# Two batches' scan blocks per burst of small products, from the fifth block on

## The chip, the cores and the metric

One core of one Trainium2 chip. The metric is the device time of one execution in microseconds (us), as the median over the executions of a kernel. The profile is of one execution; its span is some 2 us shorter than the device time. A program on one core has no second die to compare with. Of six timed executions of a kernel here often one is 2 to 4 us longer than the rest, for some kernels with a mean granted TensorE clock of 0.995 to 0.996 in place of 1.0; medians are little touched by them. One run in all was far slower: of the seven executions of the kernel before that were timed with probe, moved and late, one took 443.3 us at a mean clock of 0.852; it is marked slow and left out of the ratios. In the lines shown, PE is TensorE's passes, PEld its weight loads, DVE VectorE, ACT ScalarE, POOL GpSimd, SP SyncE.

## The reference, cut to what matters

A chunked scan (Mamba-2 style) over 4 batches, 8 heads, 768 tokens, head width 32 and state width 16, followed by a feed-forward layer with an ELU between its two large products. All fp32.

```python
for c in range(nc):                      # chunks of 32 in the reference, 64 in the kernel
    cum = np.cumsum(la, axis=-1)
    L = np.exp(cum[:, :, :, None] - cum[:, :, None, :]) * causal
    M = np.einsum('bhin,bhjn->bhij', Cc, Bc) * L             # "scores", weighed
    y_intra = np.einsum('bhij,bhjd->bhid', M, xc)            # "inside"
    y_inter = np.einsum('bhin,bhnd->bhid', Cc, state) * np.exp(cum)[..., None]   # "across"
    state = decay_full * state + np.sum(Bx, axis=2)          # "sums", "states"
# then, on x of 3072 tokens by 256:
h = x @ w_in                                                 # 256 -> 2048, called l1 below
g = np.where(h > 0, h, np.exp(np.minimum(h, 0)) - 1)         # elu
out = g @ w_out                                              # 2048 -> 256, called l2 below
```

## The kernel before: the parts that the change and the argument touch

The 3072 tokens are 12 blocks of 256. The large products (l1 and l2) of one block are interleaved with the small products of the scan of a later block. A group of l1 or of l2 is eight large passes. Each block has bursts of small products: scores (16 products of 32 rows by 64 columns of the array), sums (12 or 16, on 64 by 32), across (12 or 16, on 32 by 64) and inside (32, on 64 by 32). An fp32 product shows in the trace as two weight loads and two passes, so 16 products are "x32". A turn transposes B and C of a block by four more passes, and a bank here is the buffer that one of TensorE's output tiles takes; a large group waits where another engine has yet to read it (0.40 us for VectorE at 51.59 us in the changed kernel).

```python
def scores(n):
    gs = [psum([P, 2, 2, Q], "ps_g") for _ in range(4)]
    for u in range(2):
        for v in range(2):
            for q in range(4):
                rows, toks = slice(32 * q, 32 * q + 32), slice(Q * v, Q * v + Q)
                nc.tensor.matmul(out=gs[q][toks, u], lhsT=s["bt"][rows, u, toks],
                                 rhs=s["ctm"][rows, u, :, toks], ...)
# ... cut: sums, states, across, inside are built alike, one block at a time
def meet(n):
    across(n)
    inside(n)
    if n + 1 < NP:
        sums(n + 1)
        states(n + 1)
# ... cut
for n in range(2, NP):
    for i in range(8):
        l2(n - 2, i)
        l1(n, i)
        while lag:
            elu()
        # ... cut: loads, decays, turns of block n + 2, block 3's special case
        if i == 6 and n + 1 < NP:
            meet(n + 1)
        if i == 7 and n + 2 < NP:
            scores(n + 2)
            for q in range(4):
                weigh(n + 2, q)
```

## Time and profile before

| | before |
|---|---|
| device time, median | 390.22 us (3 runs, 390.02 to 393.0) |
| profiled span | 388.0 us |
| large passes of TensorE | 1536, 215.8 ns each: 331.5 us |
| first to last large pass | 370.9 us, so 39.6 us go to everything else in between |

The prediction below shows the lines on TensorE. What the other engines do in time is in the busy tenths of the 40 slices (9 is 90% or more of a slice of 9.7 us):

```profile
DVE  4877867943323232323123233223232321221000
ACT  3969879662653563563554464455366234334000
```

The reader is to see that VectorE (DVE) is 60% to over 90% busy only in slices 2 to 8 (some 10 to 78 us), where it also converts the weights; this is where a change of its load can reach TensorE. Behind that it is some 20 to 40% busy.

The blocks of 256 instructions that the prediction and the runs speak of: on the page 28 packets of 16 KB went over the instruction queue, and the trace records 7193 instructions of TensorE, 257 to a packet. In the changed kernel the last three of its 28 packets start behind 6553, 6809 and 7065 recorded instructions, so 256 apart. A packet takes 0.88 to 1.45 us, 1.01 in the median.

A way of reading that carries this whole document: the large passes are the same in every version, so I add up, pass by pass, how much longer than 215.8 ns it took from each large pass to the next. Everything that a burst, a wait or a stop costs is in that sum, called **lost time** below. A burst's cost is the gap that it leaves plus 0.104 us, by which the second large pass behind any burst comes late.

### The profile page before, as it was taken

What the parts mean: (1) busy time and instruction counts of PE and PEld (TensorE: products, weight loads), DVE (VectorE), ACT (ScalarE), POOL (GpSimd) and SP (SyncE); (2) the same over time, 40 slices, a digit from 0 to 9 for tenths busy, and PEclk for the clock granted to TensorE, in tenths of its full rate; (3) what the DMA queues carried; (4) which work ended last, traced back from release to release, by engine and by line L of the source; (5) the groups of instructions that cost most, each with busy time, mean ns of one, the idle gap of its engine ahead of it and who ended that gap; (6) DMA issues with size and microseconds to landing.
All of it is one profiled execution on the core that took longest, in us unless ns stands there. A gap on an engine that the chain in (4) does not pass through costs nothing.

```text
span 388.0 us, 8744 instructions
## 1 busy us (share of the span) xinstructions
PE 381.7 (98%) x3546; PEld 323.8 (83%) x3546; DVE 136.8 (35%) x280; ACT 200.1 (52%) x480; POOL 73.0 (19%) x133
## 2 busy tenths in 40 slices
PE   8999999999999999999999999999999999999996
PEld 4678788888888888888888888888888888888885
DVE  4877867943323232323123233223232321221000
ACT  3969879662653563563554464455366234334000
POOL 6525426540120120011021012012012000000000
DMA  8979966016007007006105303402500000000000
GB/s 165 225 165 256 280 157 119 7 37 113 4 12 133 7 3 137 14 2 123 28 0 88 65 0 53 101 0 45 95 2 29 2 0 11 20 2 27 0 29 27
DMA packets 86921, 25.02 MB, mean 64 GB/s; under 512 B 77184, under 2 KB 81504, under 8 KB 86880
## 3 DMA queue, kind: packets, MB, share of 16 engines
q1 hardware_dynamic: 84704, 24.26, 29.7%
q8 instruction: 28, 0.46, 0.5%
q10 hardware_dynamic: 2176, 0.20, 0.4%
q14 instruction: 13, 0.11, 0.1%
HBM read 21.10 MB, written 3.34 MB: 63 GB/s over the span
## 4 chain that ended last, share of the span: by engine, by line
PE 83%; ACT 5%; DMA 3%; SPq 3%; DVE 3%; issue 1%; POOL 0%; DVEq 0%; ACTq 0%; POOLq 0%
PE ps_o L552 38%; PE ps_h L525 36%; PE ps_o L567 4%; PE ps_y L497 2%; ACT L L393 2%; SPq L107 2%; PE ps_g L412 1%; DMA w<-in_moe_w_in_dram 1%; PE ps_y L482 1%; DMA xr<-in_x_dram 1%; ACT e L537 1%; DMA flat<-F 1%; PE ps_st L438 1%; ACT mag L152 1%; SPq L115 1%
## 5 line engine op out<-in xcount | busy, mean ns | idle before, releaser
L525 PE MATMUL ps_h<-yT,w_in 128*128 128x256 f32 x768 | 181.3, 380 | 1.1 <-DVE g L539 0.5
L552 PE MATMUL ps_o<-w_out,g 128*128 128x256 f32 x704 | 167.3, 382 | 0.1
L525 PEld LDWEIGHTS ps_h<-yT,w_in 128*128 128x128 f32 x768 | 145.5, 190 | 22.0 <-ACT yT L508 0.9
L552 PEld LDWEIGHTS ps_o<-w_out,g 128*128 128x128 f32 x704 | 131.7, 190 | 19.5 <-issue 1.4
L539 DVE SCALAR_TENSOR_TENSOR g<-e,ps_h 128x512 f32<-128x512 f32 x96 | 65.9, 687 | 209.7 <-ACT e L538 209.6
L537 ACT ACTIVATE e<-ps_h 128x512 f32<-128x512 f32 x96 | 57.1, 595 | 137.2 <-PE ps_h L525 137.0
L538 ACT ACTIVATE e<-e 128x512 f32<-128x512 f32 x96 | 60.5, 630 | 3.0
L398 POOL TENSOR_SCALAR_AFFINE_SELECT L<-L 64x512 f32<-64x512 f32 x40 | 26.6, 665 | 132.4 <-ACT L L393 131.2
L393 ACT ACTIVATE L<-L,ncum 128x64 f32<-128x64 f32 x160 | 41.9, 334 | 0.0
L508 ACT COPY yT<-ps_y 64x128 f32<-64x128 f32 (+1 forms) x70 | 17.9, 260 | 6.7 <-PE ps_y L497 5.7
L459 POOL TENSOR_TENSOR Sx<-S_new,hmask 128x64 f32<-128x64 f32 x44 | 13.3, 304 | 20.8 <-DVE S_new L454 14.1
L421 DVE TENSOR_TENSOR M<-ps_g,L 128x256 f32<-128x256 f32 x48 | 17.1, 416 | 0.1
L558 ACT COPY ob<-ps_o 128x512 f32<-128x512 f32 x11 | 6.4, 585 | 18.4 <-PE ps_o L552 18.4
L321 POOL TENSOR_TENSOR sc<-bc,eb 128x256 f32<-128x256 f32 x12 | 7.8, 656 | 38.9 <-DMA bc<-in_B_dram 37.2
L567 PE MATMUL ps_o<-w_out,g 128*128 128x256 f32 x64 | 14.0, 379 | 0.0
L567 PEld LDWEIGHTS ps_o<-w_out,g 128*128 128x128 f32 x64 | 12.2, 190 | 1.6
L194 POOL TENSOR_TENSOR w_out<-mag,w_out 128x512 uint32<-128x512 uint32 x8 | 10.2, 1274 | 16.5 <-DVE mag L184 16.5
L194 POOL TENSOR_TENSOR w_in<-mag,w_in 128x512 uint32<-128x512 uint32 x8 | 10.2, 1277 | 15.2 <-DVE mag L184 15.2
L184 DVE SCALAR_TENSOR_TENSOR mag<-mag,sgn 128x512 uint32<-128x512 uint32 x16 | 12.3, 772 | 0.5
L454 DVE SCALAR_TENSOR_TENSOR S_new<-S_new,ec,ps_st 128x64 f32<-128x64 f32 x40 | 11.2, 279 | 2.5
L152 ACT ACTIVATE mag<-w 128x512 f32<-128x512 f32 x16 | 10.7, 671 | 1.5 <-DMA w<-in_moe_w_in_dram 1.3
L497 PE MATMUL ps_y<-M,xr 64*32 64x64 f32 x768 | 10.6, 225 | 0.0
(67 smaller groups left out, 137.5 us busy)
## 6 DMA issues: line engine op xcount, KB each, us to landing
L<-flat SPq DMA_DIRECT2D x20, 256.0 KB, 4.5
w<-in_moe_w_in_dram SPq DMA_DIRECT2D x8, 512.0 KB, 5.0
w<-in_moe_w_out_dram SPq DMA_DIRECT2D x8, 512.0 KB, 6.4
xr<-in_x_dram SPq DMA_DIRECT2D x24, 128.0 KB, 4.4
out_dram<-ob SPq DMA_DIRECT2D x11, 256.0 KB, 2.2
bc<-in_B_dram SPq DMA_DIRECT2D x24, 64.0 KB, 3.2
bc<-in_C_dram SPq DMA_DIRECT2D x22, 64.0 KB, 3.4
ec<-flat_exp SPq DMA_DIRECT2D x64, 16.0 KB, 1.8
```

The source lines that it names most:

```text
L194: nc.gpsimd.tensor_tensor(out=w, in0=w_mag[i][:, :, cols], in1=w, op=ALU.add)
L393: nc.scalar.activation(L[:, h, u], L[:, h, u], ACT.Exp, bias=ncum[:, u, row:row + 1])
L398: nc.gpsimd.affine_select(out=part, in_=part, pattern=[[0, 4], [0, 2], [1, Q]], compare_op=ALU.is_ge, fill=0.0, base=0, channel_multiplier=-1)
L421: nc.vector.tensor_tensor(out=M, in0=s["g"][q], in1=s["L"][:, 2 * q:2 * q + 2].rearrange("p k u i -> p u k i"), op=ALU.mult)
L497: nc.tensor.matmul(out=s["y"][t][v][col:col + D, u], lhsT=s["x"][toks, u, D * h:D * (h + 1)], rhs=s["M"][h // 2][toks, u, h % 2], start=Fa ...
L508: nc.scalar.copy(out=yT[n][at:at + count, t, :, Q * v:Q * v + Q], in_=s["y"][t][v][src:src + count])
L525: nc.tensor.matmul(out=ps[:, j], lhsT=w_in[:, k, m * P:(m + 1) * P], rhs=yT[n][:, k].rearrange("p u i -> p (u i)"), start=(k == 0), stop=( ...
L537: nc.scalar.activation(e, ps, ACT.Relu, scale=-1.0)
L538: nc.scalar.activation(e, e, ACT.Exp, scale=-1.0)
L539: nc.vector.scalar_tensor_tensor(out=g_of[n][:, 2 * i:2 * i + 2], in0=e, scalar=1.0, in1=ps, op0=ALU.subtract, op1=ALU.max)
L552: nc.tensor.matmul(out=o_of[n][:, ts], lhsT=g_of[n][:, m, ts * P:(ts + 1) * P], rhs=w_out[:, m], start=(m == 0 and ts == 0), stop=(m == MC ...
L567: nc.tensor.matmul(out=ps, lhsT=g_of[n][:, m, ts * P:(ts + 1) * P], rhs=w_out[:, m], start=(m == 0), stop=(m == MC - 1))
```

## The change

Its intent: fewer edges. A burst of small products costs TensorE time at its two ends (0.33 us in the kernel before) and at each change of tile shape inside it (0.14 to 0.19 us); blocks 4 to 11 are taken as four pairs of two batches at the same position, with one burst for scores and sums of both and one for across and inside of both. The places of the second burst are set by hand in a table ("placed by the count of TensorE's instructions"). The diff, cut to its core:

```diff
+    def place(n):
+        return 2 * (n // (2 * NG)) + n % 2, n // 2 % NG      # two batches side by side
-    def scores(n):
+    def scores(*ns):
-        s["g"] = gs = [psum([P, 2, 2, Q], "ps_g") for _ in range(4)]
+        gs = [psum([P, len(ns), 2, 2, Q], "ps_g") for _ in range(4)]
+        for at, n in enumerate(ns):
     # ... cut: the same for sums, across, inside
-    def meet(n): ...
-            first_exp(3)                       # block 3's exponent as a product
+            spread_exp(3)                      # ... by DMA (issued earlier, s == 8)
+    ends = {(3, 14): 4, (5, 10): 6, (7, 13): 8, (9, 9): 10}
+    def end_of_two(n, step):
+        m = ends.get((n, step))
+        if m:
+            inside(across(m, m + 1), m, m + 1)
     # ... cut: order of loads and turns
+            if 4 <= m < NP and n % 2 == 1:
+                if i == 2:
+                    scores(m, m + 1)
+                    sums(m, m + 1)
+                    for q in range(4):
+                        weigh(m, q)
+                        weigh(m + 1, q)
+                    states(m)
+                    states(m + 1)
+            end_of_two(n, 2 * i + 1)
```

By the new numbering block 1 is the first block of the second batch (before, the second block of the first), and block 2 has four chunks to sum where it had three.

More of the change, by code (lines that the diff above doesn't have):

```diff
@@ L70 @@
     const = ctx.enter_context(tc.tile_pool(name="const", bufs=1))
-    raw = ctx.enter_context(tc.tile_pool(name="raw", bufs=4))
+    raw = ctx.enter_context(tc.tile_pool(name="raw", bufs=3))
     att = ctx.enter_context(tc.tile_pool(name="att", bufs=2))
@@ L95 @@
     st = {}
+    def place(n):
+        return 2 * (n // (2 * NG)) + n % 2, n // 2 % NG
     def rows_of(n):
-        b, g = divmod(n, NG)
+        b, g = place(n)
         return slice(BH * g + NH * b, BH * g + NH * (b + 1))
     def load_bc(n, c_queue=nc.sync):
-        b, g = divmod(n, NG)
+        b, g = place(n)
         st.setdefault(n, {})["bc"] = raw.tile([P, 2, 2, NH, N], F32, tag="bc", name="bc")
@@ L110, in load_x @@
     def load_x(n):
-        b, g = divmod(n, NG)
-        st[n]["x"] = raw.tile([P, 2, NH * D], F32, tag="xr", name="xr")
+        b, g = place(n)
+        st[n]["x"] = raw.tile([P, 2, NH * D], F32, tag="xr", name="xr", bufs=4)
         for u in range(2):
@@ L150, in w_abs @@
     def w_abs(i):
-        w_mag[i] = conv.tile([P, 2, CW], U32, tag="mag", name="mag", bufs=3)
+        w_mag[i] = conv.tile([P, 2, CW], U32, tag="mag", name="mag")
         nc.scalar.activation(w_mag[i].bitcast(F32), w_words(i)[1].bitcast(F32), ACT.Abs)
@@ L198 @@
     w_load(0)
-    idle = const.tile([P, 4, P], BF16, name="idle")
+    idle = att.tile([P, 4, P], BF16, tag="M", name="idle", bufs=8)
     nc.vector.memset(idle, 0.0)
@@ L242 @@
         out=minus, in0=ident, scalar1=-1.0, scalar2=None, op0=ALU.mult)
-    heads = [const.tile([ROWS, NH, N], F32, name=f"heads{n}") for n in range(4)]
-    for n in range(4):
+    heads = [const.tile([ROWS, NH, N], F32, name=f"heads{n}") for n in range(3)]
+    for n in range(3):
         nc.gpsimd.tensor_copy(
@@ L400, in decay @@
                     compare_op=ALU.is_ge, fill=0.0, base=0, channel_multiplier=-1)
-    def scores(n):
-        s = st[n]
-        s["g"] = gs = [psum([P, 2, 2, Q], "ps_g") for _ in range(4)]
-        for u in range(2):
-            for v in range(2):
-                for q in range(4):
-                    rows, toks = slice(32 * q, 32 * q + 32), slice(Q * v, Q * v + Q)
-                    nc.tensor.matmul(
-                        out=gs[q][toks, u], lhsT=s["bt"][rows, u, toks],
-                        rhs=s["ctm"][rows, u, :, toks], start=True, stop=True,
-                        tile_position=(32 * q, Q * v), skip_group_check=True)
-        s["M"] = []
+    def scores(*ns):
+        gs = [psum([P, len(ns), 2, 2, Q], "ps_g") for _ in range(4)]
+        for at, n in enumerate(ns):
+            s = st[n]
+            for u in range(2):
+                for v in range(2):
+                    for q in range(4):
+                        rows, toks = slice(32 * q, 32 * q + 32), slice(Q * v, Q * v + Q)
+                        nc.tensor.matmul(
+                            out=gs[q][toks, at, u], lhsT=s["bt"][rows, u, toks],
+                            rhs=s["ctm"][rows, u, :, toks], start=True, stop=True,
+                            tile_position=(32 * q, Q * v), skip_group_check=True)
+            s["g"], s["M"] = [g[:, at] for g in gs], []
     def weigh(n, q):
@@ L426, in chunks, with sums @@
     def chunks(n):
-        return [(u, v) for u in range(2) for v in range(2) if n % NG < NG - 1 or u + v < 2]
-    def sums(n, pool=p_a, tag="a"):
-        s = st[n]
-        s["st"] = ps = [psum([P, 2, 2 * D], "ps_st"),
-                        pool.tile([P, 2, 2 * D], F32, tag=tag, name="ps_st")]
-        for u, v in chunks(n):
-            toks = slice(Q * v, Q * v + Q)
-            for q in range(4):
-                nc.tensor.matmul(
-                    out=ps[v][32 * q:32 * q + 32, u],
-                    lhsT=s["sc"][toks, u, 2 * q:2 * q + 2].rearrange("p h n -> p (h n)"),
-                    rhs=s["x"][toks, u, 2 * D * q:2 * D * (q + 1)], start=True, stop=True,
-                    tile_position=(Q * v, 32 * q), skip_group_check=True)
+        return [(u, v) for u in range(2) for v in range(2)
+                if place(n)[1] < NG - 1 or u + v < 2]
+    def sums(*ns, pool=p_a, tag="a"):
+        ps = [psum([P, len(ns), 2, 2 * D], "ps_st"),
+              pool.tile([P, len(ns), 2, 2 * D], F32, tag=tag, name="ps_st")]
+        for at, n in enumerate(ns):
+            s = st[n]
+            for u, v in chunks(n):
+                toks = slice(Q * v, Q * v + Q)
+                for q in range(4):
+                    nc.tensor.matmul(
+                        out=ps[v][32 * q:32 * q + 32, at, u],
+                        lhsT=s["sc"][toks, u, 2 * q:2 * q + 2].rearrange("p h n -> p (h n)"),
+                        rhs=s["x"][toks, u, 2 * D * q:2 * D * (q + 1)], start=True, stop=True,
+                        tile_position=(Q * v, 32 * q), skip_group_check=True)
+            s["st"] = [p[:, at] for p in ps]
     def states(n):
-        b, g = divmod(n, NG)
+        b, g = place(n)
         s = st[n]
@@ L456, in states @@
                     in1=add, op0=ALU.mult, op1=ALU.add)
-            Sx = att.tile([P, 2, D], F32, tag="Sx", name="Sx", bufs=8)
+            Sx = att.tile([P, 2, D], F32, tag="Sx", name="Sx", bufs=12)
             nc.gpsimd.tensor_tensor(
@@ L462, in states, with across @@
             at = 2 * u + v + 1
-            starts[n + at // 4, at % 4 // 2, at % 2] = Sx
+            starts[n + at // 4 * 2, at % 4 // 2, at % 2] = Sx
     def shift(n, v):
         return 2 * D * v if n else 0
-    def across(n):
-        s = st[n]
-        s["y"] = y = [[psum([P, 2, Q], "ps_y") for _ in range(2)] for _ in range(2)]
+    def across(*ns):
+        y = [[psum([P, len(ns), 2, Q], "ps_y") for _ in range(2)] for _ in range(2)]
         for u in (1, 0):
-            for v in range(2):
-                Sx = starts.pop((n, u, v), None)
-                if Sx is None:
-                    continue
-                for q in range(4):
-                    rows, col = slice(32 * q, 32 * q + 32), (64 * q + shift(n, v)) % P
-                    nc.tensor.matmul(
-                        out=y[q // 2][v][col:col + 64, u],
-                        lhsT=Sx[rows].rearrange("p k d -> p (k d)"),
-                        rhs=s["cts"][rows, u, Q * v:Q * v + Q], start=(u == 1), stop=False,
-                        tile_position=(32 * q, col), skip_group_check=True)
@@ L488, in inside @@
-    def inside(n, ts=(0, 1)):
-        s = st[n]
-        for t in ts:
-            for u in range(2):
+            for at, n in enumerate(ns):
                 for v in range(2):
-                    toks = slice(Q * v, Q * v + Q)
+                    Sx = starts.pop((n, u, v), None)
+                    if Sx is None:
+                        continue
                     for q in range(4):
-                        h, col = 4 * t + q, (D * q + shift(n, v)) % P
+                        rows, col = slice(32 * q, 32 * q + 32), (64 * q + shift(n, v)) % P
@@ L497, in inside @@
                         nc.tensor.matmul(
-                            out=s["y"][t][v][col:col + D, u],
-                            lhsT=s["x"][toks, u, D * h:D * (h + 1)],
-                            rhs=s["M"][h // 2][toks, u, h % 2], start=False, stop=True,
-                            tile_position=(Q * v, col), skip_group_check=True)
-            if t == 0:
-                yT[n] = ffn.tile([P, KC, 2, P], F32, tag="yT", name="yT")
+                            out=y[q // 2][v][col:col + 64, at, u],
@@ new lines, in across, with inside @@
+                            lhsT=Sx[rows].rearrange("p k d -> p (k d)"),
+                            rhs=st[n]["cts"][rows, u, Q * v:Q * v + Q],
+                            start=(u == 1 and at == 0), stop=False,
+                            tile_position=(32 * q, col), skip_group_check=True)
+        return y
+    def inside(y, *ns):
+        for t in range(2):
+            for at, n in enumerate(ns):
+                s = st[n]
+                for u in range(2):
+                    for v in range(2):
+                        toks = slice(Q * v, Q * v + Q)
+                        for q in range(4):
+                            h, col = 4 * t + q, (D * q + shift(n, v)) % P
+                            nc.tensor.matmul(
+                                out=y[t][v][col:col + D, at, u],
+                                lhsT=s["x"][toks, u, D * h:D * (h + 1)],
+                                rhs=s["M"][h // 2][toks, u, h % 2], start=False, stop=True,
+                                tile_position=(Q * v, col), skip_group_check=True)
+            n = ns[0]
+            if n // 2 not in yT:
+                yT[n // 2] = ffn.tile([P, KC, 2, 2, P], F32, tag="yT", name="yT")
+            out = yT[n // 2][:, t, n % 2:n % 2 + len(ns)]
@@ L508, in inside @@
                     nc.scalar.copy(
-                        out=yT[n][at:at + count, t, :, Q * v:Q * v + Q],
-                        in_=s["y"][t][v][src:src + count])
-        if 1 in ts:
+                        out=out[at:at + count, :, :, Q * v:Q * v + Q],
+                        in_=y[t][v][src:src + count])
+        for n in ns:
             st.pop(n)
@@ L526, in l1 @@
                     out=ps[:, j], lhsT=w_in[:, k, m * P:(m + 1) * P],
-                    rhs=yT[n][:, k].rearrange("p u i -> p (u i)"),
+                    rhs=yT[n // 2][:, k, n % 2].rearrange("p u i -> p (u i)"),
                     start=(k == 0), stop=(k == KC - 1))
@@ L541, in elu, with row_of @@
             op0=ALU.subtract, op1=ALU.max)
+    def row_of(n):
+        b, g = place(n)
+        return b * S + g * BLK
     o_of = {}
@@ L558, in l2 @@
             nc.scalar.copy(out=ob, in_=o_of.pop(n))
+            r0 = row_of(n)
             nc.sync.dma_start(
-                out=out[n * BLK:(n + 1) * BLK, :].rearrange("(t p) e -> p t e", p=P), in_=ob)
+                out=out[r0:r0 + BLK, :].rearrange("(t p) e -> p t e", p=P), in_=ob)
     def l2_last(n):
@@ L571, in l2_last @@
             nc.scalar.copy(out=ob[:, ts], in_=ps)
-            r0 = n * BLK + ts * P
+            r0 = row_of(n) + ts * P
             nc.sync.dma_start(out=out[r0:r0 + P, :], in_=ob[:, ts])
-    def meet(n):
-        across(n)
-        inside(n)
-        if n + 1 < NP:
-            sums(n + 1)
-            states(n + 1)
     def w_take(i, low):
@@ L619 @@
     turn_exp(0)
-    sums(0, p_o, "o")
+    sums(0, pool=p_o, tag="o")
     first_minus(*first)
@@ L634 @@
         weigh(0, q)
-    nc.gpsimd.tensor_copy(F[3 * BH:4 * BH, 0], F[BH:2 * BH, 0])
-    second = (1, 0, 1), (1, 1, 3)
+    second = (1, 0, 0), (1, 1, 3)
     first_low(1, 0)
@@ L641 @@
     w_low(1, nc.scalar)
-    across(0)
-    inside(0)
+    inside(across(0), 0)
     w_sign(1)
@@ L672 @@
     scores(1)
-    sums(1, p_o, "o")
+    sums(1, pool=p_o, tag="o")
     weigh(1, 0)
@@ L681 @@
     w_take(4, nc.vector)
-    across(1)
-    inside(1)
+    inside(across(1), 1)
     ncum = turned(F[0:ROWS, 0], "ncum", -1.0, nc.vector)
@@ L714 @@
             load_x(3)
+            spread_exp(3)
             weigh(2, 2)
             weigh(2, 3)
-            sums(2, p_o, "o")
+            sums(2, pool=p_o, tag="o")
             states(2)
         if s == 10:
-            across(2)
-            inside(2)
+            inside(across(2), 2)
         if len(lag) > 1:
             elu()
-    spread_exp(4)
+    ends = {(3, 14): 4, (5, 10): 6, (7, 13): 8, (9, 9): 10}
[3 more added lines that the diff above has]
+            inside(across(m, m + 1), m, m + 1)
     for n in range(2, NP):
@@ L730 @@
                 w_take(todo, nc.vector)
+            end_of_two(n, 2 * i)
             l1(n, i)
@@ L737 @@
                 elu()
-            if i == 0:
-                if n + 2 < NP:
-                    load_bc(n + 2)
-                    spread_cum(n + 2)
-                    load_x(n + 2)
-                if n + 3 < NP:
-                    spread_exp(n + 3)
             if n == 2:
@@ L757 @@
                         weigh(3, q)
-            if n + 2 < NP:
-                if i == 1:
-                    scaled(n + 2, nc.gpsimd)
-                if i == 3:
-                    turn(n + 2)
-                    turn_exp(n + 2)
-                if 2 <= i < 6:
-                    decay(n + 2, i - 2)
-            if i == 4 and n == 2:
-                sums(3)
-                states(3)
-            if i == 6 and n + 1 < NP:
-                meet(n + 1)
-            if i == 7 and n + 2 < NP:
-                scores(n + 2)
-                for q in range(4):
-                    weigh(n + 2, q)
+                if i == 4:
+                    sums(3)
+                    states(3)
+            if n == 2 and i == 6:
+                inside(across(3), 3)
+            m = n + 2 + n % 2
+            if 4 < m < NP and n % 2 == 1 and i in (4, 5):
+                spread_cum(m + i - 4)
+            m = n + 2 - n % 2
+            if 4 <= m < NP and n % 2 == 0:
+                if i < 2:
+                    if m == 4:
+                        spread_cum(m + i)
+                    load_bc(m + i)
+                    spread_exp(m + i)
+                if i == 2:
+                    load_x(m)
+                    load_x(m + 1)
+                if i >= 2:
+                    decay(m + i // 6, (i - 2) % 4)
+                if i in (5, 7):
+                    turn(m + i // 7)
+                    turn_exp(m + i // 7)
+            if 4 <= m < NP and n % 2 == 1:
+                if i < 2:
+                    decay(m + 1, i + 2)
+                    scaled(m + i, nc.gpsimd)
+                if i == 2:
+                    scores(m, m + 1)
+                    sums(m, m + 1)
+                    for q in range(4):
+                        weigh(m, q)
[3 more added lines that the diff above has]
+            end_of_two(n, 2 * i + 1)
     for i in range(8):
```

## The prediction

> **What bounds the kernel now.** I read the page's engine totals first, then the chain that ended last, then the waits of the two TensorE rows in the steady part (88 to 357 us), then TensorE's timeline there.
>
> ```profile
> PE 381.7 (98%) x3546; PEld 323.8 (83%) x3546; DVE 136.8 (35%) x280; ACT 200.1 (52%) x480; POOL 73.0 (19%) x133
> PE   8999999999999999999999999999999999999996
> ...
> PE 83%; ACT 5%; DMA 3%; SPq 3%; DVE 3%; issue 1%; POOL 0%; DVEq 0%; ACTq 0%; POOLq 0%
> ```
>
> TensorE is busy in every slice and the chain is TensorE for 83%; no other engine is above 52%. A busy TensorE may still wait inside, so the waits of its weight loads between 88 and 357 us:
>
> ```profile
> PEld ps_y L482 <- issue: 2.6, 8, 0.3
> PEld ps_g L412 <- issue: 2.3, 7, 0.3
> PEld ps_o L552 <- issue: 1.2, 7, 0.2
> ```
>
> That is the whole list: nobody waits for another engine, a DMA or a buffer (the matmul row itself lists no wait at all). Each of these stops is at an edge between the large products and the small ones. The timeline of one steady period (start, length, line, shapes, passes):
>
> ```profile
> 128.99 1.89 PE L525 MATMUL ps_h<-yT,w_in 128*128 128x256 f32 x8
> 130.71 0.38 PE L331 MATMUL ps_tb<-ident,bc 128*128 128x128 f32 x2
> 130.93 0.38 PE L331 MATMUL ps_tc<-ident,bc 128*128 128x128 f32 x2
> 131.15 1.89 PE L552 MATMUL ps_o<-w_out,g 128*128 128x256 f32 x8
> 132.88 1.89 PE L525 MATMUL ps_h<-yT,w_in 128*128 128x256 f32 x8
> ...
> 139.79 1.89 PE L525 MATMUL ps_h<-yT,w_in 128*128 128x256 f32 x8
> 141.61 0.49 PE L482 MATMUL ps_y<-cts,Sx 32*64 32x64 f32 x32
> 142.02 0.89 PE L497 MATMUL ps_y<-M,xr 64*32 64x64 f32 x64
> 142.71 0.52 PE L438 MATMUL ps_st<-xr,sc 64*32 64x64 f32 x32
> 143.15 2.00 PE L552 MATMUL ps_o<-w_out,g 128*128 128x256 f32 x8
> 144.99 1.89 PE L525 MATMUL ps_h<-yT,w_in 128*128 128x256 f32 x8
> 146.81 0.69 PE L412 MATMUL ps_g<-ctm,bt 32*64 32x128 f32 x32
> ```
>
> A group of eight large passes takes 1.727 us (131.15 to 132.88), so 215.8 ns a pass. What a burst of small products costs is the distance of the large groups around it less two groups. The meeting (across, inside, sums): 144.99 - 139.79 - 3.454 = 1.75 us. The scores: the next L525 group starts at 149.26, so 149.26 - 144.99 - 3.454 = 0.82 us. The turn: 132.88 - 128.99 - 3.454 = 0.44 us. Two more cases, a meeting without sums and sums alone:
>
> ```profile
> 322.96 1.89 PE L525 MATMUL ps_h<-yT,w_in 128*128 128x256 f32 x8
> 324.78 0.49 PE L482 MATMUL ps_y<-cts,Sx 32*64 32x64 f32 x32
> 325.20 0.89 PE L497 MATMUL ps_y<-M,xr 64*32 64x64 f32 x64
> 326.01 1.99 PE L552 MATMUL ps_o<-w_out,g 128*128 128x256 f32 x8
> 327.84 1.89 PE L525 MATMUL ps_h<-yT,w_in 128*128 128x256 f32 x8
> ...
> ```
>
> Meeting without sums: 327.84 - 322.96 - 3.454 = 1.43 us, so sums behind inside add 0.32. Sums alone (L525 groups at 70.79 and 74.82): 4.03 - 3.454 = 0.58 us. The same 16 products thus cost 0.26 us more when they have edges of their own. The edges, from single starts in the trace: the first small product comes 0.31 us after the last large one instead of 0.216 (0.09 lost); between across and inside, where the tile changes from 32 rows by 64 columns to 64 by 32, the next start waits 0.145 (some 0.14 lost); from inside to sums, same tile, 17 ns; after the last small one the first large pass waits 0.15 (0.20 after scores) and the second comes 0.104 late. So in and out cost about 0.33, a change of tile inside a burst 0.14 to 0.19.
>
> [...] 0.14 us at the change of tile, 17 ns where only the data changes. [...] The page shows an instruction queue with 28 packets and 0.46 MB, 16 KB each, 0.5% of 16 engines' 388 us, so 1.1 us each; no burst of before shows a stall from it. [...]
>
> **The change part by part.** Order of instructions and diff say that the large products (1536 passes, 331.5 us) stay. Blocks 0 to 3 run singly as before. Blocks 4 to 11 become four pairs of two batches at the same position, each with one burst scores+sums and one burst across+inside: two bursts per pair for four.
>
> Before, blocks 4 to 11: eight scores at 0.82 = 6.55; meetings 4 to 11 at 1.66, 1.75, 1.75, 1.66, 1.75, 1.75, 1.66 (sums of three chunks: 0.09 less) and 1.43 = 13.4; block 4's sums behind meeting 3, 0.32. Together 20.25 us.
>
> After, scores+sums of a pair: in 0.09; single scores take 0.42 to the last start, and each further round of eight passes 0.109, four more for the second block: 0.86; change of tile 0.20; sums alone take 0.385 from first start to the next large one, plus 0.32 for the second block, plus 0.10 late second pass. Sum 1.96; pairs 4 and 10 have three chunks, 1.78. Across+inside: 1.43, plus four more rounds of across at 0.058 = 0.23, plus 64 more inside passes at 10.6 ns = 0.68: 2.34. Four pairs: 2*1.96 + 2*1.78 + 4*2.34 = 16.85 us. Gain 3.40 us.
>
> Block 3's exponent comes by DMA, so two passes of L311 go: its turn costs 0.87 (62.62 - 58.29 - 3.454), a turn without them 0.44; gain 0.43. Block 2 sums four chunks instead of three: loss 0.09. Turns, transposes and large products: none. Total 3.74 us, all on the path, as TensorE sets the end.
>
> Beside other work: copies of y double in width but halve in number (six of about 0.36, the mean of a 128x256 copy, for twelve of 0.26): ScalarE is freer. The copy of F (0.48, GpSimd) and one of heads (0.45) go, in the start, where TensorE hardly waits for them (0.3 us in the waits). Fewer buffers (bc 3, mag 2): the sum that frees a mag ends about a step before the second next one wants it (POOL sum at 67.6 to 68.9, ACT abs at 71.2), so no wait.
>
> **The rivals.** (1) VectorE's queue after the pair burst becomes the bound. It does 8 weighings of 0.416 and up to 8 states of 0.279, 5.6 us in a row behind one elu that ends some 2.1 us after the burst's start: 7.7 us. The shortest distance to across is the last pair's: 1.96 + four groups of 1.73 = 8.7 us, and that pair has 6 states (7.1, with the last mask on GpSimd 7.6). Margin about 1 us; the banks for the l1 groups in between come free by 5.5. If it failed, up to 1 us lost, in one pair. (2) Instruction fetch: across+inside of a pair is 96 products, each two loads and two passes, 384 instructions in 2.2 us; a burst of before has at most 256. If a whole block of 256 lies in it (1.6 us at this rate), a fetch that takes 1.1 us after being asked for and issued may come late, by my estimate up to 0.4 us, at most 1.6 over four pairs. Counting after's instructions, the bursts start at 0.83, 0.20, 0.89 and 0.13 of a block (origin unknown): near one phase, so the author has placed them to avoid it, as the title says. I give it 0.15 us. (3) DMA: L, bc, ec of two blocks come together, ec's 8 small ones in 5 to 6 us of SyncE; 16 us for a pair of which the last is wanted 24 us after. DMA is busy for 26% there. Hidden. In the third block of steps (53 to 80 us), where VectorE is 90% busy, a late ec of block 3 could hold VectorE's queue: up to 1 us. (4) The gain could be larger if single bursts pay a ramp that a double one does not: at most some tenths.
>
> **Range and chances.** 390.22 - 3.74 + 0.15 = 386.6 us. If every edge saving is halved and one rival takes 0.5 it is 388.5; if all goes well and the start gains 0.7 it is 385.5. For 2% faster TensorE would have to save 7.8 us; the bursts of blocks 4 to 11 are 20 us in all and their products stay, so 2%. For 2% slower a new wait of 11 us would be needed: 2%.
>
> **What would show it.** Right: eight bursts in the steady part; scores+sums 1.9 to 2.0 (1.8), across+inside 2.3 to 2.4 us by the same subtraction; the "issue" waits of L482's and L412's successors in number halved; turn of block 3 at 0.44; span near 384.3. Wrong: a wait of across for the GpSimd mask or VectorE, gaps inside a burst with no releaser (fetch), a first l1 of a pair waiting for ScalarE's yT, or a start (to 53 us) that moves by more than 0.5 us.

## The result, and the profile after

The changed kernel took 387.91 us in the median of 6 runs (387.49 to 388.39), before 390.35 us (6 runs, 390.02 to 393.0). Ratios are computed from the mean time of one kernel's fast runs over that of the other's fast runs of the same rounds, so they are not quite the ratio of the medians quoted: 0.9926, 95% interval 0.9899 to 0.9953. That is faster by 0.7%, "same" at the mark of 2%, and inside the predicted range, 1.3 us above the predicted time. The profiled span is 385.5 us.

First the page's totals and the chain that ended last:

```profile
PE 378.7 (98%) x3544; PEld 324.1 (84%) x3544; DVE 136.9 (36%) x280; ACT 196.7 (51%) x455; POOL 72.1 (19%) x131
...
PE 88%; ACT 4%; DMA 3%; SPq 3%; issue 1%; DVE 0%; ACTq 0%
```

TensorE was busy for 381.7 us and is for 378.7; it still sets the end. Then the waits of the weight loads between 88 and 357 us (waited for, total, times, longest), which is again the whole list, and the matmul row has none:

```profile
PEld ps_y L490 <- issue: 1.3, 4, 0.3
PEld ps_g L417 <- issue: 1.3, 4, 0.3
PEld ps_st L445 <- POOL sc L325: 0.7, 4, 0.2
```

At the way into a burst there are eight stops in place of 15. The third line names GpSimd, and the scaled B tile of the pair's second block had indeed been ready for only 0.10 us (96.68 us, the load starts at 96.78). But in gs_single (below) the first load of sums stands still for the same 0.17 us where its block's tile had been ready for 6.9 us, so this stop belongs to the change of tile from scores to sums (0.198 us from the last score's start to the first sum's). No engine, DMA or buffer holds TensorE up here, though GpSimd has only that 0.10 us to spare, so rivals 1 and 3 of the prediction did not bite in the steady part. TensorE's timeline there:

```profile
93.83 1.89 PE L538 MATMUL ps_h<-yT,w_in 128*128 128x256 f32 x8
95.65 1.21 PE L417 MATMUL ps_g<-ctm,bt 32*64 32x128 f32 x64
96.78 0.72 PE L445 MATMUL ps_st<-xr,sc 64*32 64x64 f32 x48
97.44 1.99 PE L569 MATMUL ps_o<-w_out,g 128*128 128x256 f32 x8
99.27 1.89 PE L538 MATMUL ps_h<-yT,w_in 128*128 128x256 f32 x8
...
109.63 1.89 PE L538 MATMUL ps_h<-yT,w_in 128*128 128x256 f32 x8
111.36 1.89 PE L569 MATMUL ps_o<-w_out,g 128*128 128x256 f32 x8
113.17 0.99 PE L490 MATMUL ps_y<-cts,Sx 32*64 32x64 f32 x64
114.10 1.51 PE L508 MATMUL ps_y<-M,xr 64*32 64x64 f32 x128
115.54 1.99 PE L538 MATMUL ps_h<-yT,w_in 128*128 128x256 f32 x8
```

By the subtraction of the prediction, scores and sums of pair 4 cost 99.27 - 93.83 - 3.454 = 1.99 us (predicted 1.78). From the single starts, all eight bursts:

| burst | predicted | measured, pairs 4, 6, 8, 10 |
|---|---|---|
| scores + sums | 1.78 or 1.96 | 1.99, 2.12, 2.12, 1.99 |
| across + inside | 2.34 | 2.56, 2.40, 2.56, 2.48 |
| all eight | 16.85 | 18.22 |

Block 2's across and inside is the other place where the two traces differ from what was foreseen. Before:

```profile
49.95 0.49 PE L482 MATMUL ps_y<-cts,Sx 32*64 32x64 f32 x32
50.36 0.88 PE L497 MATMUL ps_y<-M,xr 64*32 64x64 f32 x64
51.28 1.99 PE L525 MATMUL ps_h<-yT,w_in 128*128 128x256 f32 x8
```

After, the same lines:

```profile
49.88 0.49 PE L490 MATMUL ps_y<-cts,Sx 32*64 32x64 f32 x32
50.30 0.88 PE L508 MATMUL ps_y<-M,xr 64*32 64x64 f32 x64
51.59 1.99 PE L538 MATMUL ps_h<-yT,w_in 128*128 128x256 f32 x8 [0.40 <-DVE g L552]
```

The bracket is idle time and its releaser: the next large group waits 0.40 us for a bank that VectorE's elu product frees. VectorE's rows say why. Before:

```profile
47.39 0.91 DVE L454 SCALAR_TENSOR_TENSOR S_new<-S_new,ec,ps_st 128x64 f32<-128x64 f32 x3
```

After:

```profile
47.30 1.30 DVE L462 SCALAR_TENSOR_TENSOR S_new<-S_new,ec,ps_st 128x64 f32<-128x64 f32 x4
```

One state more lies in VectorE's queue ahead of the elus. Where the 2.47 us of lost time (39.56 to 37.09 us) came from:

| place | gain, us | predicted |
|---|---|---|
| blocks 4 to 11, bursts: 20.25 to 18.22 | 2.03 | 3.40 |
| block 3's exponent by DMA: turn 0.87 to 0.44 | 0.43 | 0.43 |
| a wait at 76.3 us for GpSimd that is gone, with its late second pass | 0.33 | not foreseen |
| block 1's across, 4 products fewer | 0.05 | not foreseen |
| block 2's sums, one chunk more | -0.03 | -0.09 |
| block 2's across+inside, waiting for VectorE | -0.37 | not foreseen |
| sum | 2.44 of 2.47 | 3.74 |

The trace of before names the wait at 76.3 us:

```profile
PEld ps_o L552 <- POOL w_out L194: 0.5, 1, 0.5
```

The first load of an l2 group waits for a piece of w_out, of which GpSimd's last step ends at 76.73 us. In the changed kernel the same step ends at 75.87 us; two products of a turn (1.0 us from 71.72 us on), which stood ahead of this piece on VectorE before, come behind it there (from 78.76 us on). That this order is the whole reason was not tested.

So two questions are open: why are the pairs' bursts 1.37 us dearer than the sum of their parts, and is the hand-made placing needed at all?

### The profile page after: what moved, and what is told of

It reads as the page before. It is cut to its first block, busy times and chain, and to the rows that moved or that the text cites. A ratio compares the mean times of both kernels' runs of the same rounds, so it can differ in the third digit from the quotient of the medians.

```text
span 385.5 us, 8666 instructions
## 1 busy us (share of the span) xinstructions
PE 378.7 (98%) x3544; PEld 324.1 (84%) x3544; DVE 136.9 (36%) x280; ACT 196.7 (51%) x455; POOL 72.1 (19%) x131
## 4 chain that ended last, share of the span: by engine, by line
PE 88%; ACT 4%; DMA 3%; SPq 3%; issue 1%; DVE 0%; ACTq 0%
PE ps_o L569 40%; PE ps_h L538 38%; PE ps_o L585 4%; PE ps_y L508 2%; SPq L111 2%; PE ps_g L417 1%; DMA w<-in_moe_w_in_dram 1%; PE ps_y L490 1%; ACT L L397 1%; DMA xr<-in_x_dram 1%; PE ps_st L445 1%; DMA flat<-F 1%; ACT e L550 1%; SPq L119 1%; ACT mag L156 1%
## 5 line engine op out<-in xcount | busy, mean ns | idle before, releaser
L521 ACT COPY yT<-ps_y 64x256 f32<-64x256 f32 (+3 forms) x46 | 14.3, 318 | 9.8 <-PE ps_y L508 9.3
L508 PE MATMUL ps_y<-M,xr 64*32 64x64 f32 x768 | 9.6, 225 | 0.0
L342 DVE TENSOR_TENSOR ctm<-ps_tc,hmask 128x512 f32<-128x512 f32 x12 | 8.2, 684 | 3.8 <-PE ps_tc L335 3.8
```

The costliest lines, as they stand in the source:

```text
L508: nc.tensor.matmul(out=y[t][v][col:col + D, at, u], lhsT=s["x"][toks, u, D * h:D * (h + 1)], rhs=s["M"][h // 2][toks, u, h % 2], start=Fal ...
```

## The experiments

Twelve runs were made, ten of new kernels and two of the changed one again; all gave correct results. probe, moved2, gs_single and ai_single are single looks, whose state is unknown; only the times inside their traces carry the argument, not their device times. Theory **Q**: the first 32 passes of a burst start faster than those behind them (in the across of the changed kernel's pair 8 the 32nd pass starts 0.270 us behind the first, the 64th 0.775), whatever the place of the burst. A single block's phases have 32 passes and just fit, a pair's have 64 and pay. That the cause is a queue of instructions was my guess; no run shows it. Theory **F**: TensorE's instruction fetch comes late where many small instructions are consumed in a short time, and the placing avoids it. Theory **V**: block 2's 0.37 us are VectorE's one state more.

### probe: the burst by itself, in many lengths

Behind the finished kernel, bursts of 8, 16, 24, 32 and 64 small products in the tile form of across and then in that of inside, each behind eight large products; then 32 products behind 1, 2 and 4 large ones; then bf16; then one burst shaped like a pair's. The outputs stay right, the tail is extra.

```diff
+    for k in (8, 16, 24, 32, 64):
+        large(8)
+        small_a(k)                 # 32 rows by 64 columns; small_i: 64 by 32
+    ...
+    for k in (1, 2, 4):
+        large(k)
+        small_a(32)
+    for k in (16, 32, 64):
+        large(8)
+        small_a(k, ident16)        # bf16
```

> The changed kernel with bursts of small products of 8, 16, 24, 32 and 64 products (two passes each) appended behind its end, each between eight large products (16 passes), in the form of across (32 rows by 64 columns) and of inside (64 by 32); then across bursts of 32 behind only 1, 2 and 4 large products; then bf16 bursts (one pass a product) of 16, 32 and 64; then across 32 and inside 64 in one burst. Output correct, time longer by the tail. Theory Q [...] the first 32 passes of every burst start about 7 ns apart and the later ones [...] 11 to 17 ns a pass: the kink stands at pass 32 or so in both forms and for bf16 too (at product 32), and comes earlier behind 1 large product. Theory E (edges alone, as predicted): 7.3 ns a pass in the across form and 10.6 ns in the inside form from end to end, no kink. Theory F (instruction fetch): pauses whose place has nothing to do with the pass count.

Measured (466.41 us with the tail, one look). Cost of a burst with its edges, us:

```
passes        16     32     48     64    128
across form  0.497  0.613  0.906  1.040  1.720
inside form  0.469  0.581  0.851  0.985  1.612
bf16         0.394  0.457         0.833
starts of the across form, ns behind the first, every 8th pass, then the last:
0, 107, 165, 224, 292 | 459, 539, 605; 697
```

In both fp32 forms 16 more passes cost 0.11 to 0.12 us up to 32 passes and 0.27 to 0.29 us for the next 16: the slope jumps at pass 33. Up to there passes start some 7 ns apart (58 ns per eight), then comes a pause, and behind it 8 to 17 ns. The same kink stands at 32 passes in bf16 (3 to 4 ns a pass up to there, 8.3 behind), where a product is one load and one pass. As 32 passes are 32 products there and 16 in fp32, it isn't the number of products that counts; it is 32 passes, or 64 instructions with their loads, which these runs cannot tell apart. Theory Q stands for the pace; why it falls there was not shown. The detail that the kink would come earlier behind a single large product fell: 64 passes cost 1.041, 1.039, 1.040 and 1.041 us behind 2, 4, 8 and 16 large passes, so two large passes ahead are enough for the same cost. The composite burst at the end showed 32 fast passes again behind the change of tile (0.146 us from start to start there), and, unasked for, a stop of 2.16 us followed by large passes 426 ns apart in place of 215.8, half the pace (the mean granted clock of this execution was 0.996): theory F's kind of stop, at which the next runs look.

### moved and moved2: other places for the pairs' second burst

```diff
-    ends = {(3, 14): 4, (5, 10): 6, (7, 13): 8, (9, 9): 10}
+    ends = {(3, 10): 4, (5, 14): 6, (7, 9): 8, (9, 13): 10}      # moved
+    ends = {(3, 12): 4, (5, 12): 6, (7, 11): 8, (9, 11): 10}     # moved2
```

> The four across+inside bursts moved by four steps (64 of TensorE's instructions, a quarter of a 256-instruction fetch block): steps 10, 14, 9, 13 for 14, 10, 13, 9. Theory Q: each burst costs what it did, 2.56, 2.40, 2.56, 2.48 us within 0.1; span 385.5 within 0.5. Theory F: with a whole fetch block inside the burst, each pays up to 0.4 us more, span up to 387. A third thing it could show: VectorE not ready for the burst at step 9, up to 1 us in one burst.

> The same four bursts at steps 12, 12, 11, 11, an eighth of a fetch block from both earlier placements. Theory Q: 2.4 to 2.6 us each, as in the changed kernel. Theory F: somewhere between the changed kernel and the one moved by four steps, or the worst of the three; bursts differ by their place, not by their number of passes.

moved took 394.85 us (4 runs, 393.02 to 395.81) against 390.91 of before, ratio 1.0098 (1.006 to 1.0137): slower than the kernel before. moved2 took 392.7 in its one look. Theory Q alone, by which only the bursts' make-up counts, fell here. The second across+inside burst of moved:

```profile
175.10 0.83 PE L490 MATMUL ps_y<-cts,Sx 32*64 32x64 f32 x48
175.86 1.37 PE L508 MATMUL ps_y<-M,xr 64*32 64x64 f32 x114
178.78 0.34 PE L508 MATMUL ps_y<-M,xr 64*32 64x64 f32 x14 [1.55 <-issue]
179.06 3.28 PE L538 MATMUL ps_h<-yT,w_in 128*128 128x256 f32 x7
```

After 114 of 128 passes TensorE stops, and "issue" means that it waits for nothing the profile knows. The large passes behind it (seven in 3.28 us, where eight take 1.89 elsewhere) run at half the pace for 3.5 us; the mean granted clock of this execution was 0.996. Seven of these eight bursts have such a stop inside or in the first large passes behind, of 0.47 to 1.77 us in moved and 0.79, 1.38 and 2.13 in moved2. Numbering the recorded instructions of TensorE, every one of them, and probe's, stands at the same remainder, index 193 modulo 256, and ends 1.2 to 1.5 us after the end of a 16 KB packet of the instruction queue. The bursts that stopped began 156 to 233 or 255 instructions behind such a boundary (one at 134); the clean one of moved2 began at 9; those of the changed kernel, all clean, at 31, 124, 42 and 102.

### shifted: same places, other count

Moved and moved2 change the time of the burst and the count together. This kernel changes only the count: 90 more TensorE instructions, tiny idle products at the very start.

```diff
-    idle_products(7)
+    idle_products(4)
+    for _ in range(48):
+        nc.tensor.matmul(out=ps_idle[:, 0, 0:32], lhsT=idle[:, 0], rhs=idle[:, 0, 0:32],
+                         start=True, stop=True)
```

> The changed kernel with its pair bursts at their own places, but with TensorE's instruction count moved: 3 of the 7 idle products at the very start are dropped and 48 tiny ones put in, so 90 more instructions stand ahead of all bursts. Counted from the index 193 modulo 256 at which every stop stood so far, the four across+inside bursts of 384 instructions (the second 352) started at 31, 124, 42 and 102 in the changed kernel (none stopped), and start at 121, 214, 132 and 192 here. Theory F (an instruction fetch comes late where a burst runs over two such boundaries, that is from a start behind 128 on): the first burst keeps its 2.56 us, the second, third and fourth stop for 0.5 to 2.1 us each, behind the first boundary or at the second; time 388 + 1.5 to 6 us, so slower than the changed kernel by 1.5 us at least, and near before or above it. Rival T (the stops of moved and moved2 belong to their times in the kernel, for instance to other transfers there): nothing changes, 388.0 us within 0.6, all four bursts within 0.1 us of those of the changed kernel.

393.43 us (4 runs, 392.38 to 393.87), ratio to before 1.0074 (1.0052 to 1.0097). The first large pass starts at 13.63 us (13.68 in the changed kernel), so the idle products themselves cost nothing. Waits of the weight loads between 88 and 357 us:

```profile
PEld ps_y L511 <- issue: 3.9, 3, 1.7
PEld ps_y L493 <- issue: 1.3, 4, 0.3
PEld ps_g L420 <- issue: 1.3, 4, 0.3
PEld ps_h L541 <- issue: 1.0, 1, 1.0
PEld ps_st L448 <- POOL sc L328: 0.7, 4, 0.2
```

The first and fourth line are new against the changed kernel. The third pair's burst, at 232.9 us in the changed kernel:

```profile
232.91 0.99 PE L490 MATMUL ps_y<-cts,Sx 32*64 32x64 f32 x64
233.83 1.51 PE L508 MATMUL ps_y<-M,xr 64*32 64x64 f32 x128
235.28 0.92 PE L569 MATMUL ps_o<-w_out,g 128*128 128x256 f32 x3
```

and in the shifted one:

```profile
234.40 0.99 PE L493 MATMUL ps_y<-cts,Sx 32*64 32x64 f32 x64
235.32 1.49 PE L511 MATMUL ps_y<-M,xr 64*32 64x64 f32 x126
238.38 0.30 PE L511 MATMUL ps_y<-M,xr 64*32 64x64 f32 x2 [1.57 <-issue]
```

The bursts start at 120, 213, 131 and 191 behind the boundary. The second, third and fourth stop for 0.54, 1.85 and 1.59 us, all at the next boundary but one; the first burst itself is clean (2.451 us of gap, 2.455 in the changed kernel), but at 120 + 384 = 504 instructions it ends just short of that boundary, and the large passes behind it stop there for 1.00 us. Together 4.98 us, and the lost time rose from 37.09 to 42.07 us: nothing else changed. So the count decides, not the time: rival T falls and theory F stands. That it is the fetch that comes late rests on the packet of the instruction queue that ended 1.2 to 1.5 us ahead of each stop's end in moved, moved2 and probe. The rule of these runs: all twelve stops (moved, moved2, shifted, probe) end a block of 256 instructions that TensorE, without the stop, ran through in 1.5 to 2.4 us. Speed alone doesn't decide: two blocks that took 2.2 us were crossed without a stop (in probe at 427.0 us, in shifted at 220.7 us), and what tells these apart stays open. A burst of 384 instructions holds a full block if it starts more than 128 behind a boundary (those at 131 and 134 stopped); one that ends just short of the second boundary leaves the stop to the large passes behind it (starts at 120, and at 156 with 352 instructions). The four of the changed kernel start at 31 to 124 and end at least 26 short of it. Nor does a stop's length alone decide whether the large passes behind it are slow: they were at 426 ns behind the 1.77 us in moved, but at the full pace (six in 1.56 us) behind 1.79 us between two starts in the third burst here, with a mean granted clock of 1.0.

### gs_single and ai_single: one half of the pairing undone

```diff
-                if i == 2:
-                    scores(m, m + 1)
-                    sums(m, m + 1)
+                if i in (2, 3):                      # gs_single
+                    scores(m + i - 2)
+                    sums(m + i - 2)
-            inside(across(m, m + 1), m, m + 1)
+            inside(across(m), m)                     # ai_single; m + 1 one step later
```

> Scores+sums of a pair taken apart again into two bursts a step apart; across+inside stays paired at the same instruction counts. By the prediction's sum a single burst is 1.20, two are 2.41 against 1.96: 0.45 a pair, 1.7 us in all. By theory Q [...] two cost 2.4 to 2.7 against the measured 2.12 (1.99 for three chunks): 0.3 to 0.6 a pair, span 386.7 to 387.7.

> Across+inside of a pair taken apart into two bursts of 192 instructions with one large group between; scores+sums stay paired. By the prediction 2*1.43 against 2.34, 0.52 a pair, 2.1 us. By theory Q 2*1.43 against the measured 2.56, 2.40, 2.56, 2.48: 0.30, 0.46, 0.30, 0.38, in all 1.4 us, span 386.9. Theory F: no pause, as no two block boundaries lie within 3.7 us.

gs_single: 389.27 us in one look; single bursts of scores and sums cost 1.279 and 1.177 us (three chunks). Two of them against the pair's 2.122 and 1.989: 0.436 and 0.365 saved, 1.60 in four pairs. ai_single: 389.38 us in one look; across and inside alone cost 1.427 each, so pairing saves 0.30, 0.46, 0.30 and 0.37, 1.43 in all. Its timeline shows what a pair avoids:

```profile
113.67 0.49 PE L490 MATMUL ps_y<-cts,Sx 32*64 32x64 f32 x32
114.09 0.88 PE L508 MATMUL ps_y<-M,xr 64*32 64x64 f32 x64
114.91 1.99 PE L538 MATMUL ps_h<-yT,w_in 128*128 128x256 f32 x8
116.83 0.49 PE L490 MATMUL ps_y<-cts,Sx 32*64 32x64 f32 x32
117.25 0.88 PE L508 MATMUL ps_y<-M,xr 64*32 64x64 f32 x64
```

A single across takes 0.42 us from its start to that of inside (113.67 to 114.09), the pair's 0.93 (113.17 to 114.10): more than twice as long for twice the work. Pairing alone is thus worth 3.03 us. That is more than the 2.03 that blocks 4 to 11 gained, because the order changed as well: with single bursts everywhere the eight blocks would cost 4 * (1.279 + 1.177) + 8 * 1.427 = 21.24 us in place of 20.25 (a sum from the two traces; no kernel with both halves undone ran). Sums behind scores need a change of tile (0.20 us), where sums behind inside followed in 17 ns; that this is all of the difference was not tested. The new order costs 0.99, pairing gains 3.03.

### late, late2: block 2's fourth state

Both take the fourth state of block 2 from ahead of its across+inside and put it behind; late puts it behind the next elu, late2 ahead of it.

```diff
         if s == 8:
-            states(2)
+            states(2, slice(0, 3))
         if s == 10:
-            inside(across(2), 2)
+            inside(across(2), 2)                 # block 2's tiles kept, not shown
+            states(2, slice(3, 4))               # late2; in late behind the elu below
         if len(lag) > 1:
             elu()
```

> The changed kernel with block 2's fourth state update (new with the change, wanted only by block 4) put behind the across+inside of block 2 instead of ahead of it on VectorE. If that update (0.28 us) is what holds TensorE behind the burst at 49.6 us (extra 1.80 us against 1.43 before, released by VectorE's g), the extra falls to 1.43 to 1.50 and the span by 0.3 to 0.4 us to about 385.15. If the wait comes from something else there, the span stays at 385.5.

> The changed kernel with one thing moved: block 2's fourth state is taken from VectorE ahead of block 2's across+inside and put directly behind it, ahead of the next elu (in the run called late it stood behind that elu). Theory V (the 0.37 us of block 2 are VectorE's one state more, in the way of an elu): the burst at 50 us falls from 1.80 us of lost time to 1.43 to 1.50, no second product waits 1.5 us for the state 3 us later, and the ratio to before is 0.001 below that of after_third in this call, that is 0.2 to 0.4 us. Rival: the wait only moves (to the next first product, whose bank elu or the state frees), as in late: then the lost time between first and last large product stays at 37.1 us.

late: 389.49 us (4 runs, 389.36 to 390.23), ratio 0.9971 (0.9946 to 0.9996). The burst at 50 us fell from 1.80 to 1.48 us of gap, as expected, and then a new wait came:

```profile
51.91 1.99 PE L538 MATMUL ps_h<-yT,w_in 128*128 128x256 f32 x8
55.45 0.89 PE L569 MATMUL ps_o<-w_out,g 128*128 128x256 f32 x3 [1.54 <-DVE S_new L462]
```

The first l2 product uses the bank in which block 2's sums lie, so it waits for the state that reads them. That state stood on VectorE behind an elu which itself waited for ScalarE:

```profile
54.42 0.69 DVE L552 SCALAR_TENSOR_TENSOR g<-e,ps_h 128x512 f32<-128x512 f32 x1 [2.57 <-ACT e L551]
55.02 0.28 DVE L462 SCALAR_TENSOR_TENSOR S_new<-S_new,ec,ps_st 128x64 f32<-128x64 f32 x1
```

A miss of mine, and the wait I moved cost more (1.71) than the one I removed (0.32). In late2 the state runs at once:

```profile
50.45 0.68 DVE L552 SCALAR_TENSOR_TENSOR g<-e,ps_h 128x512 f32<-128x512 f32 x1
51.05 0.27 DVE L462 SCALAR_TENSOR_TENSOR S_new<-S_new,ec,ps_st 128x64 f32<-128x64 f32 x1
```

The gap of the burst is 1.47 us, no new wait appears, and the lost time is 36.77 us against 37.07 of the changed kernel in the same call. In the trace theory V is shown, with its size. In time it can't be told: 387.95 us (6 runs, 387.06 to 391.11) against 388.18, ratios 0.9936 and 0.9942 with intervals of 0.003 to each side.

### best and best2: a version ahead of both

late2 plus block 2's exponent by DMA, as the change did for block 3. best issues its eight transfers behind the eighth weight piece, best2 behind the tenth.

```diff
+    spread_exp(2)              # best: behind w_load(7); best2: behind w_load(9)
...
-            first_exp(2)
```

> The changed kernel with two repairs: block 2's fourth state update behind its across+inside and ahead of the next elu on VectorE (the earlier try put it behind that elu and held l2's first product, which waits for the sums' bank), and block 2's exponent by DMA as block 3's, so that two more passes go. Expected: extra at block 2's burst 1.43 to 1.50 for 1.80 us, no wait at the first l2 group, turn of block 2 at 0.44 for 0.87 us: span 385.5 - 0.33 - 0.43 = 384.7, time 387.1. The eight instructions fewer move all later bursts by eight against the fetch blocks (23, 116, 34, 94 behind a boundary for 31, 124, 42, 102), which should stay clear. Against: the eight small DMAs push weight loads back by 4.6 us, and a late weight piece would take all of it.

> The changed kernel itself once more on this chip, for comparison with the repaired one: span near 385.5, time near 387.9, the same burst costs to 0.01 us.

> late2 with block 2's exponent by DMA as well, its eight transfers issued behind the tenth weight piece instead of behind the eighth as in best. The turn of block 2 falls from 0.87 to 0.44 (0.43 us, as it did in best and for block 3). If the stop of best's profiled execution at 42 us came from weight pieces that were issued behind the eight transfers, no such stop appears here, and all runs lie within 0.5 us: median 386.9 to 387.4, ratio 0.991. If the exponent now comes late, VectorE waits for it at the product of ps_tc and ec near 41 us and the gain is lost.

> The changed kernel as it is, for the comparison in this call: ratio 0.994, lost time 37.1 us, burst at 50 us 1.80 us.

best took 387.13 us (6 runs, 386.6 to 389.15), ratio 0.9915 (0.9898 to 0.9933); the changed kernel in the same call (after_again) 388.21 (387.82 to 390.16), ratio 0.9944 (0.9927 to 0.9962), with the same bursts as in its first profile to 0.01 us. best2 took 387.10 us (6 runs, 386.36 to 387.66), ratio 0.9907 (0.9878 to 0.9937), against 388.18 (387.56 to 390.64), ratio 0.9942 (0.991 to 0.9974), of after_third. The turn of block 2 fell from 0.87 to 0.44 us in both. By the medians both versions are 1.1 us ahead of the changed kernel; the intervals of the ratios overlap.

Of best's six runs the profiled one is the slow one, 389.15 us. The gap around block 2's scores, at 41.9 us, is 2.70 us there (1.33 in best2), and the eight large passes behind it take 3.05 us (1.97 in best2); the mean granted clock of this execution was 0.995. VectorE's row ahead of it shows that a weight piece had landed late:

```profile
33.96 0.43 DVE L165 TENSOR_SCALAR w_in<-w 128x512 f32<-128x512 uint32 x1 [0.49 <-DMA w<-in_moe_w_in_dram]
```

best2, whose transfers queue behind two more weight pieces, shows no such stop, and none of its six runs is beyond 387.66, though they spread by 1.3 us where 0.5 was expected. That fits the weights being held up by the exponent's transfers, but the changed kernel without those transfers has one long run in six as well (390.16, 390.64), so the cause stays open.

## Why the prediction was right or wrong

Point by point, by its own steps:

- **The bound.** Right: TensorE sets the end, and no wait for an engine, DMA or buffer came up in the steady part.
- **The pair's scores + sums, 1.96 (1.78).** Measured 2.12 (1.99), 0.16 to 0.21 more. In the burst of pair 6 the 64 score passes take 0.94 us from first to last start where "0.86" stood, and the sums 0.79 to the next large pass where 0.385 + 0.32 = 0.705 stood.
- **The pair's across + inside, 2.34.** Measured 2.56, 2.40, 2.56 and 2.48. This is the term that failed most: "four more rounds of across at 0.058 = 0.23". From first to last start 32 passes of across took 0.27 us before and 64 take 0.775 after, so the second half costs 0.50. The 64 more passes of inside, at "10.6 ns" from passes that were themselves behind the kink, were 0.63 where 0.68 stood. The mechanism of the gain was right and the size off: I priced the second block at the pace of the first 32 passes. The fourth rival had the ramp the wrong way round: not the single burst pays at its start, the double one pays at its end. Probe shows the same kink (16 more passes cost 0.11 to 0.12 us up to 32, 0.27 to 0.29 behind) without any of the kernel's data or buffers.
- **Block 3's exponent, 0.43.** Right to 0.01.
- **Block 2.** The sums' loss was 0.03 for 0.09. That the fourth chunk also adds a state to VectorE just ahead of the elus that free l1's banks was not seen; late2 shows 0.32 of these 0.37 us. By luck the wait for GpSimd's piece of w_out at 76.3 us went and gave nearly the same back; the prediction had not seen that either.
- **Instruction fetch.** That the bursts are placed so as to avoid it was right, and moved and shifted show it. My "up to 0.4 us" for a stop was an estimate from how long the packet takes (1.1 us by the page) and was far too small: stops were 0.47 to 2.13 us, and a shift by 90 instructions costs 4.98 us, twice the whole gain of the change. The 0.15 us set aside for it were not needed, as no burst of the changed kernel stops.
- **VectorE's queue and DMA behind the pair burst.** Rightly held to be hidden: no load or pass waits for either between 88 and 357 us.
- **The sum.** 3.74 foreseen, 2.47 measured in the lost time: 1.37 of it in the pairs' bursts, the rest small terms that nearly cancel (+0.33, +0.05, +0.06, -0.37). The range held because it allowed for half the edges' saving.

## What to carry to other kernels

In these runs the first 32 passes of across or inside started some 7 ns apart and those behind them 8 to 17 ns: price the first 32 passes and those behind them apart, measured at the length that you will have. Where a burst of more than 256 instructions could hold a whole block between two boundaries, its place in the count of TensorE's instructions was worth more than the merge itself (4.98 us against 3.03), so after any edit that moves the count look for stops with no releaser that all stand at one remainder. And when you put work more on an engine that is idle on average, look which queue it enters there and who waits behind it (VectorE's one state more cost TensorE 0.37 us).
